# Second layer's weight sums carried over into its first half tile, next-y sums moved, products reordered

## The chip, the core and the metric

The kernel runs on one core of a Trainium2 chip. The metric is the device time of one execution in microseconds (us), lower is better. PE is the matmul engine (PEld its weight loads), DVE the vector engine, ACT the scalar engine, POOL the GpSimd engine, and SP issues most transfers; POOL issues the rest. Each engine works through its own queue in order, so an instruction that waits holds up everything behind it on that engine.

## The reference

```python
def _attn_ref(q, k, v, phi):
    a = softmax(phi over the sequence)                # 4 x 8 heads, 576 tokens, 32 memory slots
    k_m, v_m = a^T k, a^T v                           # 32 x 64 each
    attn = softmax(q k_m^T / sqrt(64))
    return attn v_m

x = attn_out as (2304 tokens, 512)
h = maximum(x @ w_in, 0);  x = (h * h) @ w_out        # 512 -> 2048 -> 512
h = x @ w_in2;  g = h * tanh(softplus(h))             # 512 -> 2048
out = g @ w_out2                                      # 2048 -> 512
```

All inputs and the output are float32. So is the arithmetic: a product is made of a high part and a low part (high by high, high by low, low by high), three matmuls each.

## The kernel before

**Layer one** (up to some 411 us) has four batches `b` of two halves with 288 tokens each; a *tile* is one (b, half) and runs over 16 chunks `fc` of the hidden width in `a_tile`, in parts for the first two batches. A *step* is one chunk: six matmuls into a bank `h`, `Relu` and `Square` on ACT, a high copy `g` and the subtraction that gives its low part on DVE (L594), and, three steps later, twelve matmuls `a` of an earlier chunk. Around them, the attention of coming batches is computed in small pieces.

**Weights of layer two.** They arrive as raw words of 64 bits, 32 units (`i2` 0 to 15, then `o2` 0 to 15). The class `Fold` turns a pair of units into seven *weight sums*, each split into high and low, staged in a tile `st` and written to memory as `wf_i2` or `wf_o2` by a transfer from POOL's queue (L301). Per unit: a load from SP (L251), a `Prelu` on ACT (L264) and two bit operations on DVE (L280, L282). Per pair: some sums on DVE, and seven times a cast on ACT (L299, `st`) with a subtraction on DVE (L300). `fold.tick` is called once per chunk; it starts a unit at every second call and does two pieces (`steps.pop`) per call. `EARLY` = 22 units are prepared before the pool `Y` is closed. The rest is done in the last two tiles, and whatever is left is drained in a loop before layer two's pools are opened. A `Prelu` is placed behind the last `Relu` of the program so far (`marks["step"]`); nothing else of `Fold` is tied. The framework's scheduler sets the order of all instructions on each engine.

**Layer two** takes three groups `i` of 768 tokens (two halves of 384). It multiplies by a scheme with seven products in place of eight. In a group's *first half* 56 steps (`h_step`, six matmuls of 384 columns into `hb`; line names `ht`, `hu`, `hs`, `a` on ACT and DVE) give the hidden values after `Mish`; in its *second half* 56 steps (`b_step`, nine matmuls of 256 columns) form the seven products `j` = 0 to 6 over eight pages `k`. `cast_step` makes high and low operands (`oph`, `opl`; L1008, L1009) three steps ahead; for `j` = 0 and 4 it also makes the operand of a later product on POOL at once (L1011, L1013). Each step reads one weight sum `u`, loaded by SP (L909) into 8 buffers (16 in the second halves), in the order in which `units` lists them. `y_work` prepares the next group's input: four loads `yr` (L858), four sums on POOL (L871, L876, L880, L885) and seven pairs of casts (L863, L864), two pieces per product of the second half in the program's text.

The *hinge* below is the passage from layer one's last matmul (411.37 us) into layer two's first half.

## Time and profile before

| | us |
|---|---|
| three runs | 788.3, 791.06 (median), 792.9 |
| profiled execution, first to last instruction | 788.8 |
| PE busy in it | 739.4 |
| mean granted clock of PE | 0.974 of full |

The profile names no time around the span; the span lies within the three runs, 2.3 us under their median. An engine's idle time is read from the timeline, where the number in brackets is the idle time before an instruction and the name behind it is what ended it.

### The profile page before, as it was taken

The numbers are of one execution on the slowest core, as the hardware profiler recorded it, in microseconds if no ns is written. First come the engines' busy times: TensorE is split into PE (matmuls) and PEld (weight loads), VectorE is DVE, ScalarE is ACT, GpSimd is POOL, SyncE is SP. The second block draws the span as 40 slices with busy tenths as digits, with TensorE's granted clock in tenths as the row PEclk, the third lists the DMA queues.
The fourth block names the chain that finished last, engine by engine and source line by source line (L and its number), as shares of the span: only waits on it lengthen the run. The fifth ranks groups of instructions, "written<-read, shape, count | busy, mean of one in ns | idle before, by whom it ended". The sixth has DMA issues, their size and how long they took to land.

```text
span 788.8 us, 16341 instructions
## 1 busy us (share of the span) xinstructions
PE 739.4 (94%) x5984; PEld 700.1 (89%) x5984; DVE 526.0 (67%) x1072; ACT 427.3 (54%) x960; POOL 136.3 (17%) x176
## 2 busy tenths in 40 slices
PE   5699999999899999989996799999999999999997
PEld 4488898998778888889995799899999999999997
DVE  3979846455757678768884559774558784556683
ACT  3577856565656677756654236452436552434552
POOL 0000000011111112232232414240112140111040
PEclk8699999999999999999998999999999999999999
DMA  9992535039888676786779978789788889788881
GB/s 333 406 406 72 187 100 195 28 124 299 279 294 297 214 246 220 258 341 208 290 254 343 295 247 292 240 268 301 240 262 251 247 265 303 244 258 251 247 265 62
DMA packets 89440, 195.85 MB, mean 248 GB/s; under 512 B 9872, under 2 KB 22672, under 8 KB 89360
## 3 DMA queue, kind: packets, MB, share of 16 engines
q1 hardware_dynamic: 80400, 165.45, 64.1%
q0 software_dynamic: 8960, 29.37, 9.6%
q8 instruction: 47, 0.77, 0.4%
q14 instruction: 33, 0.27, 0.1%
HBM read 151.78 MB, written 42.99 MB: 247 GB/s over the span
## 4 chain that ended last, share of the span: by engine, by line
PE 57%; issue 24%; POOL 7%; DMA 5%; DVE 3%; ACT 3%; SPq 1%; POOLq 0%; DVEq 0%; ACTq 0%
PE hb L964 7%; PE hb L965 7%; PE hb L966 7%; POOL wf_o L301 3%; POOL wf_i L301 3%; PE a L540 3%; PE a L541 3%; PE a L542 3%; DMA raw_i<-in_moe_w_in_dram 2%; PE h L578 1%; PE h L580 1%; PE h L579 1%; PE pw L478 1%; DMA wf_o<-st 1%; DMA u<-wf_i 1%
## 5 line engine op out<-in xcount | busy, mean ns | idle before, releaser
L540 PE MATMUL a<-g,o1h 128*128 128x288 f32 x512 | 150.5, 302 | 2.5 <-DVE ys L555 1.9
L541 PE MATMUL a<-g,o1l 128*128 128x288 f32 x512 | 149.0, 299 | 0.0
L542 PE MATMUL a<-g,o1h 128*128 128x288 f32 x512 | 132.5, 298 | 4.8 <-DVE g L594 4.8
L1009 DVE TENSOR_TENSOR opl<-a,oph 128x384 fp32r<-128x384 f32 x144 | 101.2, 723 | 50.8 <-ACT oph L1008 50.5
L964 PE MATMUL hb<-ych,u 128*128 128x384 f32 x336 | 114.8, 342 | 11.8 <-ACT ht L979 7.5
L965 PE MATMUL hb<-ycl,u 128*128 128x384 f32 x336 | 114.3, 340 | 0.0
L966 PE MATMUL hb<-ych,u 128*128 128x384 f32 x336 | 111.2, 340 | 0.0
L1008 ACT CAST oph<-a 128x384 fp32r<-128x384 f32 x144 | 73.5, 513 | 66.0 <-PE b20b L1030 5.9
L540 PEld LDWEIGHTS a<-g,o1h 128*128 128x128 f32 x512 | 97.2, 190 | 8.7 <-ACT s L586 2.9
L542 PEld LDWEIGHTS a<-g,o1h 128*128 128x128 f32 x512 | 90.3, 190 | 8.6 <-DVE g L594 6.3
L541 PEld LDWEIGHTS a<-g,o1l 128*128 128x128 f32 x512 | 97.5, 191 | 0.4 <-issue 0.4
L970 ACT ACTIVATE a<-hs 128x384 f32<-128x384 f32 x72 | 37.6, 525 | 92.2 <-DVE hs L974 92.2
L578 PE MATMUL h<-ah,wp 128*128 128x288 f32 x256 | 80.6, 316 | 5.8 <-ACT wp L484 2.8
L586 ACT ACTIVATE s<-h 128x288 f32<-128x288 f32 x128 | 52.2, 410 | 56.3 <-PE h L580 52.1
L301 POOL DMA_DIRECT2D wf_i<-st x56 | 30.3, 543 | 285.5 <-DVE st L300 278.6
L580 PE MATMUL h<-ah,wp 128*128 128x288 f32 x256 | 76.4, 299 | 0.7 <-DVE wp L485 0.7
L579 PE MATMUL h<-al,wp 128*128 128x288 f32 x256 | 76.7, 300 | 0.3 <-DVE al L468 0.3
L964 PEld LDWEIGHTS hb<-ych,u 128*128 128x128 f32 x336 | 64.3, 191 | 13.0 <-ACT ht L979 7.9
L594 DVE TENSOR_TENSOR g<-s,g 128x288 fp32r<-128x288 f32 x128 | 57.3, 450 | 26.4 <-ACT g L591 25.3
L974 DVE TENSOR_TENSOR hs<-hu,hb 128x384 f32<-128x384 f32 x72 | 39.5, 552 | 46.2 <-PE hb L966 45.8
L578 PEld LDWEIGHTS h<-ah,wp 128*128 128x128 f32 x256 | 48.7, 191 | 18.4 <-ACT s L586 5.3
L965 PEld LDWEIGHTS hb<-ycl,u 128*128 128x128 f32 x336 | 64.1, 191 | 0.0
(255 smaller groups left out, 1747.8 us busy)
## 6 DMA issues: line engine op xcount, KB each, us to landing
u<-wf_i SPq DMA_DIRECT2D x168, 256.0 KB, 3.7
u<-wf_o SPq DMA_DIRECT2D x168, 256.0 KB, 3.2
...
wf_i<-st POOLq DMA_DIRECT2D x56, 256.0 KB, 4.8
wf_o<-st POOLq DMA_DIRECT2D x56, 256.0 KB, 5.3
...
```

What stands on the lines that cost most here:

```text
L301: nc.gpsimd.dma_start(wf[key][k, :, j], st.bitcast(F32).rearrange("p s o -> p (s o)"))
L540: nc.tensor.matmul(o, wh[:, c, cs], sh, start=first, stop=False)
L541: nc.tensor.matmul(o, wl[:, c, cs], sh, start=False, stop=False)
L542: nc.tensor.matmul(o, wh[:, c, cs], sl, start=False, stop=last)
L578: nc.tensor.matmul(ph, w[:, 0, hg, fs], hi[:, hg], start=(hg == 0), stop=False)
L579: nc.tensor.matmul(ph, w[:, 0, hg, fs], lo[:, hg], start=False, stop=False)
L580: nc.tensor.matmul(ph, w[:, 1, hg, fs], hi[:, hg], start=False, stop=(hg == 1))
L964: nc.tensor.matmul(ps, wh, yh[:, d], start=(j < 4 and d == 0), stop=False, **kw)
L965: nc.tensor.matmul(ps, wh, yl[:, d], start=False, stop=False, **kw)
L966: nc.tensor.matmul(ps, wl, yh[:, d], start=False, stop=end, **kw)
L1008: nc.scalar.copy(hi, x)
L1009: sub(lo, x, hi.bitcast(F32))
```

## The change

1. `EARLY` goes from 22 to 18 units. `Fold.tick` counts time in steps (`now`) and starts a unit only if its load was recorded at least `AGE` = 4 steps ago. It does one piece per call in the first tiles, then one and two in turn, where it did two.
2. Every instruction of `tick` on every engine is placed behind the last `Relu` (or, in layer two, the last `Mish`) and the last subtraction that makes a low part (`marks["step"]`, `marks["lo"]`).
3. The staging tiles of the middle tiles come from three tags in place of two.
4. The loop that drained `Fold` before layer two is gone. The open units are ticked once per step of the first half of group 0 (0.43 steps of time each), with a small new pool `cs` for staging.
5. The `u` loads are placed behind each other in the order of `units`, with the `yr` loads between them. In group 0 the loads of the next y come after steps 8, 10, 12 and 14, three of its sums after steps 24, 29 and 34 of the first half, and its casts (with the fourth sum) at every fourth step of the second half, each tied behind that step's casts.
6. The products run in the order 0, 3, 1, 2, 4, 5, 6; the output of product 3 is added up at the end of product 2. The subtractions on POOL are put off by `k` steps. Big output tiles come from a new pool `bo`.

```diff
-EARLY = 22
+EARLY = 18
+AGE = 4.0
+PROD = [0, 3, 1, 2, 4, 5, 6]
...
+        def landed(self):
+            key, u = self.order[self.started]
+            return self.now - self.when[key, u] >= AGE
+
-        def tick(self, start=True):
+        def tick(self, start=True, pops=2, took=1.0):
+            self.now += took
+            with behind(marks, "step"), behind(marks, "lo"):
+                self.work(start, pops)
+
+        def work(self, start, pops):
             todo, self.bits = self.bits, []
-            if start and self.started < self.loaded and len(self.steps) < 5:
+            if start and self.started < self.loaded and len(self.steps) < 5 and self.landed():
...
-            for _ in range(2):
+            for _ in range(pops):
                 if self.steps:
                     self.steps.pop(0)()
...
-                nc.vector.tensor_sub(sl, s, sh.bitcast(F32))
+                marks["lo"] = nc.vector.tensor_sub(sl, s, sh.bitcast(F32))
...
-    def stage_y(n):
-        return Y.tile([P, 2, 256], F32R, tag=f"ys{2 + n // 2 % 2}", name=f"st{n}", bufs=2)
+    def stage_y(half):
+        def f(n):
+            pool, tag = ((Y, "ys2"), (Y, "ys3"), (X, f"ys{1 - half}"))[n // 2 % 3]
+            return pool.tile([P, 2, 256], F32R, tag=tag, name=f"st{n}", bufs=2)
+        return f
...
-                    fold.tick(start=fc % 2 == 0)
+                    fold.tick(pops=1)
...
-            fold.tick(start=fc % 2 == 0)
+            fold.tick(pops=1 + fc % 2)
...
+        if i:
+            sums = [s for s, _ in (sum1, sum2, sum3)]
+            last = [c for _, c in (sum1, sum2, sum3)]
+            return work, sums, last + [
+                lambda: cast(2, r[0, 1]), lambda: (cast(4, r[1, 0]), sum4()),
+                lambda: cast(6, r[1, 1]), lambda: cast(5, r[1, 0])]
...
-        units += [("o2", k, j) for j in range(7) for k in range(NPG)]
+        units += [("o2", k, j) for j in PROD for k in range(NPG)]
...
-            nc.sync.dma_start(t.bitcast(F32).rearrange("p s o -> p (s o)"), wf[key][k, :, j])
+            with behind(marks, "unit" if n else None):
+                marks["unit"] = nc.sync.dma_start(
+                    t.bitcast(F32).rearrange("p s o -> p (s o)"), wf[key][k, :, j])
...
-    while fold.busy():
-        fold.tick()
     flush()
     run_pend(0)
-    close(cm_cv)
...
+    cm_cs, CS = open_pool("cs", "right")
+    def stage_cs(n):
+        pool, tag, bufs = (CS, "stg2", 2) if n % 5 in (1, 3) else (CV, "stg", 3)
...
         if j == 0:
-            nc.gpsimd.tensor_sub(x, g[k, "x1"], x)
+            at(k, lambda: nc.gpsimd.tensor_sub(x, g[k, "x1"], x))
...
+            if j == 2:
+                tmp["u3"] = big("bu3")
+                each(add, tmp["u3"], tmp["u2"])
+                x, y = banks[3]
+                each(add, t, tmp["u3"])
...
+            if i == 0 and fold.busy():
+                assert step < 40
+                fold.tick(pops=1, took=0.43)
+            if step == 0 and more:
+                loads, sums, casts = y_work(i + 1, in_g("yr", 4), in_g("yt", 2))
+            if more and 8 <= step < 16 and step % 2 == 0:
+                loads.pop(0)()
+            if more and step in (24, 29, 34):
+                sums.pop(0)()
...
-            if one == two == 0 and (i + 1) * TT < NTOK:
-                work = y_work(i + 1, in_g("yr", 4), in_g("yt", 2))
-            if two % 3 == 2 and work:
-                work.pop(0)()
+            if more and 18 <= step < 46 and step % 4 == 2:
+                casts.pop(0)()
```

What it moves, at three places. **The hinge, ACT.** `ys312` is the last copy out of layer one's banks, `st` are casts of weight sums, `ht000` and `ht010` free layer two's first banks. Before:

```order
L557 COPY ys312_5551<-a3102_4940 128x288
L299 CAST st104_5227<-ct_o2_12_5057 128x256
L299 CAST st108_5373<-raw_o2_15_5060 128x256
L299 CAST st105_5331<-ct_o2_14_5262 128x256
L299 CAST st111_5461<-ct_o2_14_5262 128x256
L299 CAST st107_5368<-raw_o2_15_5060 128x256
L299 CAST st109_5424<-raw_o2_15_5060 128x256
L299 CAST st110_5428<-ct_o2_14_5262 128x256
L979 COPY ht000_5572<-hb000_5565 128x384
```

And with the change:

```order
L568 COPY ys312_5504<-a3102_4858 128x288
L1010 COPY ht000_5527<-hb000_5520 128x384
L310 CAST st103_5529<-ct_o2_12_5306 128x256
L1010 COPY ht010_5634<-hb010_5627 128x384
L1001 ACT_TABLE_LOAD
L1001 ACTIVATE a1100_5583<-hb000_5520 128x384
L1039 CAST oph53_6215<-a1100_5583 128x384
L1001 ACTIVATE a2200_5593<-hs003_5569 128x384
L1001 ACTIVATE a1101_5704<-hb010_5627 128x384
L1039 CAST oph54_6230<-a1101_5704 128x384
L310 CAST st105_5589<-ct_o2_14_5572 128x256
```

Seven casts stood between `ys312` and `ht000`; none does now, and the last pair's seven (105 to 111) follow spread over the steps up to about the 24th.

**The hinge, SP.** `u` with numbers under 56 are the weight sums of the running first half, those from 56 on belong to the second half, `yr` are loads of the next y. Before (`u57`, `u59`, `u61` and `u63` stand just ahead):

```order
L909 DMA u65_6241<-wf_o2_103 128x512
L909 DMA u67_6245<-wf_o2_103 128x512
L909 DMA u16_5665<-wf_i2_102 128x512
L909 DMA u69_6249<-wf_o2_103 128x512
L909 DMA u71_6253<-wf_o2_103 128x512
L858 DMA yr100_6300<-y1_104 128x2x384
L909 DMA u17_5679<-wf_i2_102 128x512
```

And with the change:

```order
L934 DMA u15_5643<-wf_i2_102 128x512
L875 DMA yr100_5659<-y1_104 128x2x384
L934 DMA u16_5661<-wf_i2_102 128x512
L934 DMA u17_5679<-wf_i2_102 128x512
L875 DMA yr101_5694<-y1_104 128x2x384
L934 DMA u18_5696<-wf_i2_102 128x512
L934 DMA u19_5708<-wf_i2_102 128x512
L875 DMA yr111_5718<-y1_104 128x2x384
```

The eight loads of the second half's weights are gone from here; they now stand behind `u55`.

**Layer one, DVE.** `ct_i2_6` and `ct_i2_4` are first bit operations on freshly loaded units, `g..` with `s..` makes a step's low part, `x20` belongs to the attention. Before, around chunk 15 of tile (1, 0):

```order
L447 STREAM_TRANSPOSE x20_2636<-psc20_2623 128x288 x2
L449 TENSOR_REDUCE smx20_2639<-x20_2636 128x18
L451 TENSOR_TENSOR x20_2636<-x20_2636,smx20_2639 128x576
L280 TENSOR_SCALAR ct_i2_6_3049<-raw_i2_6_2729 128x512
L594 TENSOR_TENSOR g10_15_2578<-s10_15_2577,g10_15_2578 128x288
L485 TENSOR_TENSOR wp20_2662<-pw200_2653,wp20_2662 128x512
```

And with the change, where the next pair begins, around chunk 13 of tile (1, 1):

```order
L605 TENSOR_TENSOR g11_12_2709<-s11_12_2708,g11_12_2709 128x288
L325 TENSOR_TENSOR ct_i2_2_2337<-raw_i2_3_2246,ct_i2_2_2337 128x256
L311 TENSOR_TENSOR st10_2807<-raw_i2_3_2246,st10_2807 128x256
L605 TENSOR_TENSOR g11_13_2763<-s11_13_2762,g11_13_2763 128x288
L469 TENSOR_TENSOR x20_2617<-x20_2617,ssm20_2712 128x576
L291 TENSOR_SCALAR ct_i2_4_2849<-raw_i2_4_2340 128x512
L332 TENSOR_TENSOR ct_i2_2_2337<-ct_i2_2_2337 128x256
L311 TENSOR_TENSOR st11_2855<-raw_i2_3_2246,st11_2855 128x256
```

Unit 6 was touched in chunk 15 of tile (1, 0), two units ahead of the one that was being finished; now unit 4 is touched four chunks later, behind the step's own subtraction.

**The second half of group 0, POOL.** `a110.` are the operands of product 1, `a120.` those of product 6, `yr`/`yt` with first figure 1 or 2 the sums of group 1's and group 2's y. Before:

```order
L1011 TENSOR_TENSOR a1104_5947<-x104_6008,a1104_5947 128x384
L885 TENSOR_TENSOR yr110_6482<-yr110_6482,yt12_6615 128x768
L871 TENSOR_TENSOR yt21_8159<-yr201_7948,yr200_7895 128x768
L1011 TENSOR_TENSOR a1105_6030<-x105_6091,a1105_6030 128x384
L1011 TENSOR_TENSOR a1106_6113<-x106_6174,a1106_6113 128x384
L876 TENSOR_TENSOR yt22_8210<-yr211_8030,yt21_8159 128x768
L880 TENSOR_TENSOR yr201_7948<-yr211_8030,yr201_7948 128x768
L1011 TENSOR_TENSOR a1107_6196<-x107_6302,a1107_6196 128x384
```

And with the change:

```order
L1044 TENSOR_TENSOR a1204_5986<-a1204_5986,a1104_5961 128x384
L899 TENSOR_TENSOR yr110_5743<-yr110_5743,yt12_5926 128x768
L1044 TENSOR_TENSOR a1205_6069<-a1205_6069,a1105_6045 128x384
L1044 TENSOR_TENSOR a1206_6152<-a1206_6152,a1106_6128 128x384
L1044 TENSOR_TENSOR a1207_6244<-a1207_6244,a1107_6211 128x384
L1042 TENSOR_TENSOR a1110_7233<-x110_7296,a1110_7233 128x384
L889 TENSOR_TENSOR yt21_7482<-yr201_7310,yr200_7283 128x768
L893 TENSOR_TENSOR yt22_7542<-yr211_7334,yt21_7482 128x768
```

All eight operands of product 1 are now made ahead of any y sum of the second half, and group 2's sums stand in group 1's first half.

## Rows read from the trace of the kernel before

**Rows 1.** The page, part 1: busy us of each engine, share, instructions.
```profile
PE 739.4 (94%) x5984; PEld 700.1 (89%) x5984; DVE 526.0 (67%) x1072; ACT 427.3 (54%) x960; POOL 136.3 (17%) x176
```

**Rows 2.** Windows: stretch, length, busy time by engine, granted clock, transfer share, GB/s.
```profile
200.00:360.00 160.00, 149.57 (x1342) 134.18 (x1341) 114.07 (x277) 102.88 (x263) 35.04 (x65) 0.98 0.76 264
...
560.00:580.00 20.00, 20.00 (x116) 20.00 (x115) 11.52 (x24) 7.06 (x14) 2.04 (x2) 1.00 0.79 244
```

**Rows 3.** PE's timeline at the hinge: start, length, instruction, idle before.
```profile
423.72 0.69 PE L964 MATMUL hb<-ych,u 128*128 128x384 f32 x1 [7.54 <-ACT ht L979]
...
436.22 0.41 PE L964 MATMUL hb<-ych,u 128*128 128x384 f32 x1 [2.10 <-DMA u<-wf_i]
...
440.39 0.41 PE L964 MATMUL hb<-ych,u 128*128 128x384 f32 x1 [1.84 <-DMA u<-wf_i]
```

**Rows 4.** ACT's timeline at the hinge.
```profile
422.88 0.40 ACT L299 CAST st<-ct_o 128x256 fp32r<-128x256 f32 x1 [2.00 <-DMA wf_o<-st]
423.19 0.86 ACT L979 COPY ht<-hb 128x384 f32<-128x384 f32 x2
```

**Rows 5.** SP's timeline at the hinge: issues in a row.
```profile
414.11 2.81 SPq L909 DMA_DIRECT2D u<-wf_i  x4
416.97 7.66 SPq L909 DMA_DIRECT2D u<-wf_o  x6
426.04 0.32 SPq L909 DMA_DIRECT2D u<-wf_i  x1
426.45 4.56 SPq L909 DMA_DIRECT2D u<-wf_o  x2
```

**Rows 6.** Windows of 4 us at the hinge, columns as in the windows above.
```profile
424.00:428.00 4.00, 4.00 (x14) 4.00 (x15) 2.67 (x6) 2.75 (x6) 0.54 (x1) 0.55 1.05 410
440.00:444.00 4.00, 3.61 (x14) 3.64 (x15) 3.08 (x3) 1.17 (x3) 4.00 (x3) 0.66 1.04 390
```

**Rows 7.** PE's timeline in layer one, with idle before.
```profile
209.11 1.30 PE L542 MATMUL a<-g,o1h 128*128 128x288 f32 x4 [1.88 <-DVE g L594]
229.36 0.40 PE L540 MATMUL a<-g,o1h 128*128 128x288 f32 x1 [1.50 <-DVE ys L555]
...
344.40 0.40 PE L542 MATMUL a<-g,o1h 128*128 128x288 f32 x1 [2.37 <-DVE g L594]
```

**Rows 8.** DVE's and ACT's timelines just ahead of those gaps.
```profile
208.26 0.43 DVE L280 TENSOR_SCALAR ct_i<-raw_i 128x512 int32<-128x512 int32 x1 [3.11 <-DMA raw_i<-in_moe_w_in_dram]
...
343.12 0.40 ACT L299 CAST st<-ct_o 128x256 fp32r<-128x256 f32 x1 [2.29 <-DMA wf_o<-st]
```

**Rows 9.** Windows: group 0's second half, then group 1's.
```profile
479.50:545.50 66.00, 63.10 (x517) 62.36 (x517) 50.13 (x71) 31.43 (x62) 21.98 (x15) 1.00 0.85 270
602.50:664.60 62.10, 62.10 (x517) 62.10 (x516) 44.67 (x71) 31.18 (x62) 17.80 (x12) 1.00 0.86 268
```

**Rows 10.** Timelines of DVE, POOL and PE in group 0's second half.
```profile
481.98 0.95 DVE L864 TENSOR_TENSOR ycl<-yr,ych 128x768 fp32r<-128x768 f32 x1
...
485.44 0.54 DVE L974 TENSOR_TENSOR hs<-hu,hb 128x384 f32<-128x384 f32 x1
485.91 2.15 DVE L864 TENSOR_TENSOR ycl<-yr,ych 128x768 fp32r<-128x768 f32 x1
...
485.27 1.97 POOL L871 TENSOR_TENSOR yt<-yr,yr 128x768 f32<-128x768 f32 x1 [0.17 <-DMA yr<-y]
...
492.03 0.39 PE L1031 MATMUL b01bg<-u,opl 128*128 128x256 f32 x1 [1.21 <-DVE opl L1009]
```

**Rows 11.** Groups by line, 300 to 412 us: name, count, busy us, mean ns.
```profile
L299 ACT CAST st<-raw_o 128x256 fp32r<-128x256 f32 x29 | 12.0, 424 | 7.8 <-DMA wf_o<-st 7.0 <-DVE raw_o L282 0.7
L300 DVE TENSOR_TENSOR st<-raw_o,st 128x256 fp32r<-128x256 f32 x27 | 11.0, 418 | 3.4 <-ACT st L299 3.4
```

**Rows 12.** The page, part 6: a load with KB each, us to landing.
```profile
u<-wf_i SPq DMA_DIRECT2D x168, 256.0 KB, 3.7
```

More of the change, by code (lines that the diff above doesn't have):

```diff
@@ L205, in fields @@
                 else:
-                    x[3] = X.tile([P, 512], F32, tag="ct", name=f"ct_{key}_{u}", bufs=2)
+                    x[3] = Y.tile([P, 512], F32, tag="ct", name=f"ct_{key}_{u}", bufs=2)
                 nc.vector.tensor_scalar(
@@ L240, in __init__ @@
             self.loaded = self.started = 0
-            self.raw, self.bits, self.odd, self.steps = {}, [], {}, []
-            self.pool, self.stage, self.n = None, None, 0
+            self.raw, self.bits, self.steps, self.when = {}, [], [], {}
+            self.pool, self.stage, self.n, self.now = None, None, 0, 0.0
         def load(self, n=1):
@@ L252, in load @@
                 self.raw[key, u] = t
+                self.when[key, u] = self.now
                 self.loaded += 1
@@ L275, in fields @@
             if u % 2 == 0:
-                t = X.tile([P, 512], F32, tag="ct", name=f"ct_{key}_{u}", bufs=2)
+                t = self.pool.tile([P, 512], F32, tag="ct", name=f"ct_{key}_{u}", bufs=2)
             else:
@@ L783, in body, with tick2, f @@
     drain(lanes)
-    def tick2(fc):
-        if fc == LAG + 1:
-            fold.stage = stage_y
-        fold.tick(start=fc % 2 == 0)
+    def tick2(half):
+        def f(fc):
+            if fc == LAG + 1:
+                fold.stage = stage_y(half)
+            fold.tick(pops=1 + fc % 2)
+        return f
     b, nb = 2, 3
@@ L845, in f @@
                 extra[0] = f"ys{1 - half}"
-            fold.tick(start=fc % 2 == 0)
+            fold.tick(pops=1 + fc % 2)
         return f
@@ L857, in load @@
             c0 = i * TT + n * HT
-            nc.sync.dma_start(r[k, n], y1[:, 2 * k:2 * k + 2, c0:c0 + HT])
+            with behind(marks, "unit" if i else None):
+                nc.sync.dma_start(r[k, n], y1[:, 2 * k:2 * k + 2, c0:c0 + HT])
         def cast(j, x):
@@ L862, in cast, with t1, t2, t3 @@
                 Y2.tile([P, 2, HT], F32R, tag=f"yc{part}{j}", name=f"yc{part}{i}{j}") for part in "hl")
-            nc.scalar.copy(hi, x)
-            nc.vector.tensor_sub(lo, x, hi.bitcast(F32))
+            with behind(marks, "hi" if i else None), behind(marks, "lo" if i else None):
+                nc.scalar.copy(hi, x)
+                nc.vector.tensor_sub(lo, x, hi.bitcast(F32))
         sub = nc.vector.tensor_sub if i == 0 else nc.gpsimd.tensor_sub
         work = [lambda k=k, n=n: load(k, n) for k, n in ((0, 0), (0, 1), (1, 1), (1, 0))]
-        def sum1():
+        def t1():
             r["t1"] = tmp(f"yt{i}1")
             sub(r["t1"], r[0, 1], r[0, 0])
-            cast(0, r[0, 0])
-        def sum2():
+        def t2():
             r["t2"] = tmp(f"yt{i}2")
             sub(r["t2"], r[1, 1], r["t1"])
-            cast(3, r["t1"])
-        def sum3():
+        def t3():
             sub(r[0, 1], r[1, 1], r[0, 1])
-            cast(1, r["t2"])
         def sum4():
-            cast(4, r[1, 0])
             sub(r[1, 0], r[1, 0], r["t2"])
-        return work + [
-            sum1, sum2, sum3, lambda: cast(2, r[0, 1]), sum4,
+        sum1 = t1, lambda: cast(0, r[0, 0])
+        sum2 = t2, lambda: cast(3, r["t1"])
+        sum3 = t3, lambda: cast(1, r["t2"])
+        if i:
[4 more added lines that the diff above has]
+                lambda: cast(6, r[1, 1]), lambda: cast(5, r[1, 0])]
+        both = [lambda s=s, c=c: (s(), c()) for s, c in (sum1, sum2, sum3)]
+        return work + both + [
+            lambda: cast(2, r[0, 1]), lambda: (cast(4, r[1, 0]), sum4()),
             lambda: cast(6, r[1, 1]), lambda: cast(5, r[1, 0])]
@@ L931, in body @@
     close(cm_wo)
+    cm_cs, CS = open_pool("cs", "right")
     cm_g, G = open_pool("g", "left")
+    def stage_cs(n):
+        pool, tag, bufs = (CS, "stg2", 2) if n % 5 in (1, 3) else (CV, "stg", 3)
+        return pool.tile([P, 2, 256], F32R, tag=tag, name=f"st{n}", bufs=bufs)
+    fold.stage = stage_cs
+    big_pool = [None]
     O, L = acc_tags, ["acc0", "acc1", "acc2", "acc3"]
@@ L969, in mish @@
             g[k, name] = half_tile(f"{name}_{k}", f"{name}{i}{k}", 1)
-            nc.scalar.activation(g[k, name], x, AF.Mish)
+            marks["step"] = nc.scalar.activation(g[k, name], x, AF.Mish)
         def total(name, a):
             t = half_tile("hs", f"hs{m}", 3)
-            add(t, a, ps)
+            marks["lo"] = add(t, a, ps)
             at(1, lambda: mish(name, t))
@@ L1039, in big @@
         def big(tag, bufs=1):
-            return G.tile([P, 3 * 256], F32, tag=tag, name=f"{tag}{m}", bufs=bufs)
+            return big_pool[0].tile([P, 3 * 256], F32, tag=tag, name=f"{tag}{m}", bufs=bufs)
         def store(t, a, b):
@@ L1067, in body @@
         plan += [("h", i, k, j) for k in range(NPG) for j in range(7)]
-        plan += [("b", i, j, k) for j in range(7) for k in range(NPG)]
+        plan += [("b", i, j, k) for j in PROD for k in range(NPG)]
     AHEAD = 3
     banks, tmp, g = {}, {}, {}
-    work = []
     def in_g(tag, bufs):
@@ L1077, in body @@
         feed(now + (8 if now < 56 else 16))
+        step = now % 56
+        more = (i + 1) * TT < NTOK
         if kind == "h":
             h_step(i, one, two, banks, tmp, g)
-        else:
+            if i == 0 and fold.busy():
[7 more added lines that the diff above has]
+                sums.pop(0)()
+        else:
+            if now == 56:
+                close(cm_cs)
+                close(cm_cv)
+                cm_bo, big_pool[0] = open_pool("bo", "right")
             b_step(i, one, two, banks, tmp)
-            if one == two == 0 and (i + 1) * TT < NTOK:
-                work = y_work(i + 1, in_g("yr", 4), in_g("yt", 2))
-            if two % 3 == 2 and work:
-                work.pop(0)()
+            if more and 18 <= step < 46 and step % 4 == 2:
+                casts.pop(0)()
         run_queue()
@@ L1090, in body @@
     close(cm_g)
+    close(cm_bo)
     close(cm_y2)
```

24 lines of the change are left out of this document (10 added, 14 removed).

## The prediction

> **What bounds the kernel now.** I read the page first: PE is busy 739.4 of 788.8 us [rows 1], so only idle PE time and time at a reduced clock can be won. Next comes a table of windows over the whole span, which tells where that time lies. Up to the first weight sums of layer two the order of instructions is the same on every engine, so the start stays as it is. From 200 to 360 us PE is busy 149.57 of 160 us at a mean granted clock of 0.98 [rows 2]. At the hinge it waits long and runs slow after it [rows 3, 6]. Group 0's second half takes 66.0 us, group 1's, with as many matmuls, 62.1 [rows 9]. In the steady part of layer two PE is busy all the time, 116 matmuls in 20 us, or 0.172 us each and 1.03 us per step of six [rows 2]; nothing is to be won there. The timeline of PE with idle time in brackets then names what ended each wait, and the timelines of ACT, DVE, POOL and SP say what that engine did ahead of it.
>
> **The hinge: what goes.** PE stands still 7.54 + 2.10 + 1.84 = 11.48 us [rows 3]. The first wait is for the copy `ht`, which starts at 423.19 because a cast `st` stood ahead of it on ACT until then, waiting 2.00 us for its staging buffer, that is for a transfer of an earlier sum [rows 4], and it was not the first cast that did. The two others are for loads `u<-wf_i`: from 416.97 to 431.0 SP issued eight loads of `wf_o`, which cannot start until their sums are written, and only one load that PE needed next [rows 5]. After these waits the granted clock was 0.55 in 424 to 428 and 0.66 in 440 to 444, with PE busy 4.00 and 3.61 us [rows 6]: 4.00 x 0.45 + 3.61 x 0.34 = 3.0 us more. **Loss 14.5 us.** The change takes both causes away: no cast stands between the last copy and `ht000`, and the eight loads stand behind `u55`.
>
> **The hinge: what comes.** The last pair's work now runs beside the first 24 steps, some 25 us. On ACT these are 7 casts at 0.42, 2.9 us; on DVE 7 subtractions at 0.42 and four bit operations and four sums on as many or twice as many numbers, so at most 0.84 each, 9.7 us at most [rows 11]; on POOL seven issues, none waited for, since `wf_o` is read only from step 56 on. DVE is busy 11.52 and ACT 7.06 in 20 us of the steady first half [rows 2]: over 25 us DVE comes to 14.4 + 9.7 = 24.1, ACT to 8.8 + 2.9 = 11.7. Both fit, DVE barely. For transfers: by step 25 the loads `u11` to `u25` (15 x 0.262 MB), some ten staged sums (2.6), two stores of y1 (0.6) and four loads of y (1.6) must be through, 8.7 MB in 25.8 us, or 337 GB/s, where 390 and 410 were moved over 4 us [rows 6]. They fit as well, without room. So the cover is thin in one place: `u11` is issued only behind the stores of y1, which is where the group at 414.11 stood, 2.7 us after layer one's last matmul [rows 5]. It is wanted six steps after that matmul, at about 6 to 7 us; landing takes 3.7 us at the median [rows 12], more in a crowd. I charge 0.5 us for the copies out of layer one's banks, 1.5 for `u11` and its followers, 1 for DVE: 3.0 us. Below it lies 0.5; above, 8.8, which is the 264 GB/s of 200 to 360 us [rows 2] in place of 337: 8.7 MB then take 33 us, 7 late, and 1.8 of clock. I take the small value, since the crowd at the hinge itself reached 390. **Gain 11.5.**
>
> **Layer one.** Idle time from 200 to 360 us is 160 - 149.57 = 10.4, and the clock costs 149.57 x 0.02 = 3.0 [rows 2]. Three gaps make 5.75 of it [rows 7]. At 209.11 and 229.36 DVE stood in a first bit operation on a unit whose load had not landed (3.11 us at 208.26), with the step's own subtraction queued behind it; at 344.40 ACT stood in a cast whose staging buffer was not free, 2.29 us at 343.12 [rows 8]. The change starts a unit four steps after its load, some 9.3 us (18 matmuls of 288 columns each, at 288/384 of 0.172 us), and places its work behind the step's; the staging ring grows from four to six tiles in the middle tiles, and in the tile of the third gap the casts leave free the four chunks into which the eight loads of `u` fall. So 1.88 + 2.37 go, and with them the clock's 3.0, which in finer windows lies right behind these two: 7.25. The gap of 1.50 I leave in place: it lies at the start of tile (2, 0), whose attention now ends a step later, with its low part right ahead of the copies out of the banks; it may vanish or grow by 1.3. Of the other 4.7 us, much belongs to the attention's chains, which stay; I take 1.75. For waits that appear elsewhere, as every piece now has a fixed place in a queue, I charge 1.0. **Gain 8.0**, between 0 (every wait returns at another step) and 11.
>
> **Group 0's second half.** 66.0 - 62.1 = 3.9 us [rows 9]. POOL's sum of group 2's y (1.97 us at 485.27) and the next two stood ahead of operands of product 1, which PE waited for three times, 1.21 us the longest [rows 10], 2.90 together. While that sum ran, DVE's `ycl` with two inputs from on-chip memory took 2.15 us against 0.95 alone, but `hs`, which reads a bank, still 0.54 [rows 10]. The order now gives product 1's operands ahead of all these sums, and product 3 fills eight steps in between. **Gain 2.9**, bounds 1.5 and 3.9.
>
> The Trainium skill (SBUF — State Buffer, section "SBUF: two separate sides") says that GpSimd and VectorE share a pair of ports as an exclusive lock, held for a whole instruction, against VectorE operations with two SBUF inputs. The trace agrees, by `ycl` and `hs` above, and the rule speaks against point 5: three sums in a first half cost DVE up to 3 x (2.15 - 0.95) = 3.6 us there. In group 1's first half DVE has room for that (11.52 of 20 us). In group 0's the same three sums ran before, but without the last pair's work beside them; now DVE would come to 24.1 + 3.6 = 27.7 us in 25, which is a way into the second rival.
>
> **What costs nothing.** The order of products moves no matmul; the two additions of product 3 move to the end of product 2, eight steps before a bank of theirs is written again. Zero, 1 us either way. The casts of y (0.95 on DVE) move from the end of the first half into the products, where DVE is busy 44.67 of 62.1 us [rows 9]. Putting off POOL's subtractions costs nothing while they end two products ahead of use. The end, after the last matmul, is the same.
>
> **The sum.** 11.5 + 8.0 + 2.9 = 22.4 us, from 788.8 to 766.4 for an execution like the profiled one. That one lies 2.3 us under the median of the three runs, 791.06; from the median the sum gives 768.7, which is my forecast: **768.7**.
>
> **The rivals.**
> 1. *The forecast*: 763 to 774. For it: each cause removed has its wait in brackets, and the order shows it gone. Chance 0.62.
> 2. *Layer two's start is bound by DVE or by transfers.* Loads or `hs` come late in the first 25 steps. For it: 337 GB/s wanted, DVE at 24.1 of 25 us. Against it: 390 to 410 was moved, and two banks' worth of steps, seven, lie between a bank's end and its reuse. The hinge then keeps about 8.8 us in place of 3.0: 768.7 + 5.8 = 774.5. Chance 0.15.
> 3. *Layer one's waits return.* Casts wait for buffers or units at other steps; that term is 0: 776.7. With the second rival, 782.5. For it: one wait of about 2 us brings the slow clock with it, as at the hinge [rows 3, 6]. Chance 0.11.
> 4. *Slower.* Units' loads land later than four steps, in the tiles in which now up to 1.5 pieces a step sit in DVE's queue; each late load costs what the one at 208.26 did, 1.88 and 1.5 of clock, 3.4 us. The gain of 22.4 is gone from seven late loads on; at ten of the 32 the time is 768.7 + 34 = 802.7. Against it: even without regard to landing, two late loads stopped PE for 1.5 us and more [rows 7, 8]. Chance 0.04.
> 5. *It does not do what it says.* The scheduler might put the work back into the same places: 791. The order of the built program speaks against it at each of the three places. Chance 0.05, with all that comes out near no change.
> 6. *All goes*, and the hinge keeps 0.5: 14.5 - 0.5 + 11 + 3.9 = 28.9, 762.2. Chance 0.03.
>
> **How the numbers follow.** 768.7 is the likeliest case's. The range 760 to 780 takes in the cases 1, 2, 3 (each alone) and 6, 0.62 + 0.15 + 0.09 + 0.03 = 0.89 on paper, of which I believe 8 in 10, since the unknown costs are many. Half a per cent, about what a measurement of this kernel tells from no change, is 4 us: faster than 787 are cases 1, 2, 3 and 6, 0.91; the same 0.05; slower 0.04.
>
> **What would show it.** In the profile after: no idle PE time over 2 us between 395 and 440, and a granted clock of 1.00 there; ACT's `ht` copies right behind the last `ys`; SP without `wf_o` loads before the first half's end; no window of 200 to 360 with a clock under 1.00; group 0's second half at about 62.5 us. Wrong would be: gaps of 2 us before `u<-wf_i` or behind DVE at the hinge (rival 2), casts on ACT that wait for transfers of earlier sums ahead of a `Relu` (rival 3), first bit operations that wait for loads (rival 4).

## The result, and the profile after

The changed kernel takes **769.88 us** (median of four runs, 768.32 to 771.89), the kernel before 791.98 us (four runs, 788.30 to 793.17): ratio 0.971, 95 % interval 0.967 to 0.975. The forecast was 768.7 us, range 760 to 780. The profiled execution spans 767.9 us, before 788.8. The total was right; one of its three terms was not.

A table made from the two traces shows where the time went. A stage ends with its last matmul; "products" is a group's second half, from its first product matmul to its last; 516 matmuls start in it each time, 504 of them its own and twelve left over from the first half. The change places the loads, sums and casts of the next y in group 1 as it does in group 0.

| stage, us | before | after | gain | predicted |
|---|---|---|---|---|
| start, to three eighths of the `a` matmuls (three of eight tiles) | 174.47 | 174.22 | 0.25 | 0 |
| rest of layer one | 236.91 | 225.96 | 10.95 | 8.0 |
| hinge, to the first product matmul | 68.12 | 56.90 | 11.22 | 11.5 |
| products, group 0 | 66.23 | 65.25 | 0.98 | 2.9 |
| first half, group 1 | 56.70 | 56.70 | 0 | 0 |
| products, group 1 | 62.37 | 65.23 | -2.86 | 0 |
| group 2 | 119.09 | 119.08 | 0 | 0 |
| after the last matmul | 4.91 | 4.60 | 0.3 | 0 |
| sum | 788.8 | 767.9 | 20.85 | 22.4 |

The page of after, part 1, and windows with busy time of PE, PEld, DVE, ACT and POOL, granted clock, share of transfers and GB/s; they answer to [rows 1, 2, 6, 9]:

```profile
PE 735.2 (96%) x5984; PEld 697.3 (91%) x5984; DVE 530.3 (69%) x1072; ACT 424.1 (55%) x960; POOL 132.1 (17%) x176
...
200.00:360.00 160.00, 155.53 (x1414) 141.53 (x1415) 127.69 (x313) 111.57 (x291) 41.83 (x77) 1.00 0.81 285
...
416.00:420.00 4.00, 1.75 (x11) 1.44 (x10) 4.00 (x6) 1.43 (x3) 3.91 (x5) 1.00 1.06 394
420.00:424.00 4.00, 4.00 (x16) 4.00 (x15) 3.97 (x4) 1.72 (x4) 3.82 (x4) 0.57 1.02 381
...
457.07:522.32 65.25, 63.46 (x518) 62.63 (x518) 47.21 (x72) 33.76 (x66) 15.00 (x12) 1.00 0.88 284
579.02:644.25 65.23, 63.45 (x518) 62.65 (x518) 47.16 (x72) 33.77 (x66) 14.99 (x12) 1.00 0.83 258
700.94:763.33 62.39, 62.39 (x517) 62.19 (x516) 39.28 (x65) 29.32 (x59) 12.81 (x11) 1.00 0.68 212
```

Layer one's stretch is busy 155.53 of 160 us at full clock, where it was 149.57 at 0.98. Groups 0 and 1 both have 1.8 us of idle PE in their products, and PE's records there are 1.1 us longer; group 2, which prepares no next y, has no idle time.

The timelines at the hinge, PE, ACT and SP in turn, and the loads of `u<-wf_i` issued there (the last line is their time to landing):

```profile
418.97 0.44 PE L995 MATMUL hb<-ych,u 128*128 128x384 f32 x1 [2.25 <-DMA u<-wf_i]
...
399.54 0.70 ACT L568 COPY ys<-a 128x288 f32<-128x288 f32 x2 [0.68 <-PE a L553]
400.13 0.50 ACT L1010 COPY ht<-hb 128x384 f32<-128x384 f32 x1
...
401.22 4.16 SPq L934 DMA_DIRECT2D u<-wf_i  x5
405.43 0.43 SPq L875 DMA_DIRECT2D yr<-y  x1
...
L934 SPq DMA_DIRECT2D u<-wf_i x18: 319/320/627, 391.9 to 417.7; - x18
...
DMA to landing us min/median/max: 3.1/6.3/8.0
```

The three waits of [rows 3], 11.48 us, have become one of 2.25 us. `ht` stands right behind the last `ys`; no `wf_o` load stands among SP's before 452.06. The wait that is left ends with a load in a crowd: at the median such a load took 6.3 us here, 3.7 over the page [rows 12].

The groups of waits from 200 us to layer one's end (engine, waiting line, what ended it: us in all, times, longest). Before, 200 to 411:

```profile
DVE ct_i L280 <- DMA raw_i<-in_moe_w_in_dram: 11.9, 5, 3.1
ACT st L299 <- DMA wf_o<-st: 11.2, 9, 2.6
ACT raw_o L264 <- DMA raw_o<-in_moe_w_out_dram: 10.4, 5, 4.1
...
ACT st L299 <- DMA wf_i<-st: 6.3, 4, 3.3
```

After, 200 to 400, and then the two gaps on PE that are left, with the cast on ACT behind the first:

```profile
ACT st L310 <- DMA wf_o<-st: 6.9, 7, 1.7
...
ACT st L310 <- DMA wf_i<-st: 4.2, 2, 3.2
...
ACT raw_o L275 <- DMA raw_o<-in_moe_w_out_dram: 1.7, 1, 1.7
...
231.32 0.40 PE L551 MATMUL a<-g,o1h 128*128 128x288 f32 x1 [1.51 <-ACT g L602]
...
235.52 0.40 PE L551 MATMUL a<-g,o1h 128*128 128x288 f32 x1 [0.99 <-ACT g L602]
...
230.04 0.42 ACT L310 CAST st<-raw_i 128x256 fp32r<-128x256 f32 x1 [3.25 <-DMA wf_i<-st]
```

No wait of DVE for a raw unit is left in this list, and casts wait 11.1 us for staging where they waited 17.5. Only the first of the two gaps has such a cast behind it; ahead of the second, ACT stood 1.68 us in an operation of the attention that waited for DVE (at 234.46).

Last, group 1's product 4 on DVE, POOL and PE:

```profile
620.70 5.23 DVE L1040 TENSOR_TENSOR opl<-a,oph 128x384 fp32r<-128x384 f32 x4
...
620.86 2.09 POOL L899 TENSOR_TENSOR yr<-yr,yt 128x768 f32<-128x768 f32 x1 [0.90 <-DVE ycl L882]
622.90 3.89 POOL L1044 TENSOR_TENSOR a<-a,a 128x384 f32<-128x384 f32 x3
...
623.41 0.39 PE L1062 MATMUL b10mm<-u,opl 128*128 128x256 f32 x1 [0.79 <-DVE opl L1040]
...
628.13 0.39 PE L1062 MATMUL b12acc<-u,opl 128*128 128x256 f32 x1 [0.82 <-DVE opl L1040]
```

This is the new wait. POOL's fourth sum of y holds back three subtractions of product 4, and the four run in a row. Meanwhile DVE needs 5.23 us for four `opl`, 1.31 each, where a step is 1.07 us (nine matmuls at 58.79 / 495 us, from the windows of e9 below); elsewhere one takes 0.56.

### The profile page after: what moved, and what is told of

The parts are those of the page before. It is cut to its first block, busy times and chain, and to the rows that moved or that the text cites. A ratio compares the mean times of both kernels' runs of the same rounds, so it can differ in the third digit from the quotient of the medians.

```text
span 767.9 us, 16335 instructions
## 1 busy us (share of the span) xinstructions
PE 735.2 (96%) x5984; PEld 697.3 (91%) x5984; DVE 530.3 (69%) x1072; ACT 424.1 (55%) x960; POOL 132.1 (17%) x176
## 4 chain that ended last, share of the span: by engine, by line
PE 71%; issue 8%; DVE 7%; DMA 7%; ACT 4%; POOL 2%; SPq 0%; DVEq 0%; POOLq 0%; ACTq 0%
PE hb L995 7%; PE hb L996 7%; PE hb L997 7%; PE a L551 6%; PE a L553 5%; PE a L552 5%; PE h L589 3%; PE h L590 2%; PE h L591 2%; DMA raw_i<-in_moe_w_in_dram 2%; POOL wf_o L312 2%; PE pw L489 1%; DVE opl L1040 1%; DMA u<-wf_i 1%; DMA wf_i<-st 1%
## 5 line engine op out<-in xcount | busy, mean ns | idle before, releaser
L1040 DVE TENSOR_TENSOR opl<-a,oph 128x384 fp32r<-128x384 f32 x144 | 97.1, 690 | 47.4 <-ACT oph L1039 47.2
L995 PE MATMUL hb<-ych,u 128*128 128x384 f32 x336 | 113.8, 339 | 2.2 <-DMA u<-wf_i 2.2
L589 PE MATMUL h<-ah,wp 128*128 128x288 f32 x256 | 79.1, 310 | 5.1 <-ACT wp L495 3.1
L591 PE MATMUL h<-ah,wp 128*128 128x288 f32 x256 | 76.0, 297 | 0.7 <-DVE wp L496 0.7
L995 PEld LDWEIGHTS hb<-ych,u 128*128 128x128 f32 x336 | 63.5, 189 | 2.9 <-DMA u<-wf_i 2.6
L997 PEld LDWEIGHTS hb<-ych,u 128*128 128x128 f32 x336 | 63.4, 189 | 0.0
```

The lines of the kernel that those rows point to most:

```text
L589: nc.tensor.matmul(ph, w[:, 0, hg, fs], hi[:, hg], start=(hg == 0), stop=False)
L591: nc.tensor.matmul(ph, w[:, 1, hg, fs], hi[:, hg], start=False, stop=(hg == 1))
L995: nc.tensor.matmul(ps, wh, yh[:, d], start=(j < 4 and d == 0), stop=False, **kw)
L997: nc.tensor.matmul(ps, wl, yh[:, d], start=False, stop=end, **kw)
L1040: marks["lo"] = sub(lo, x, hi.bitcast(F32))
```

## The experiments

Ten kernels were run. Their times come from three sittings, in which the kernel before had medians of 791.9 (e1 to e4), 794.9 (e5 to e8) and 793.3 us (e9, e10), so small differences are read from the stages of the traces:

| kernel | median us | ratio to before, interval | rest of layer one | hinge | products 0 | products 1 |
|---|---|---|---|---|---|---|
| after | 769.88 | 0.971, 0.967-0.975 | 225.96 | 56.90 | 65.25 | 65.23 |
| e1 | 774.70 | 0.978, 0.972-0.983 | 227.77 | 60.41 | 65.03 | 65.24 |
| e2 | 773.63 | 0.978, 0.973-0.982 | 224.75 | 60.12 | 66.78 | 65.29 |
| e3 | 786.54 | 0.994, 0.991-0.996 | 235.69 | 62.54 | 65.26 | 65.24 |
| e4 | 768.88 | 0.971, 0.966-0.975 | 225.94 | 56.71 | 64.98 | 64.95 |
| e5 | 764.55 | 0.964, 0.960-0.968 | 226.14 | 56.86 | 63.63 | 63.38 |
| e6 | 766.66 | 0.967, 0.963-0.971 | 225.80 | 54.50 | 65.20 | 65.01 |
| e7 | 763.26 | 0.962, 0.957-0.966 | 225.80 | 54.08 | 63.61 | 63.64 |
| e8 | 758.60 | 0.956, 0.953-0.960 | 222.34 | 53.77 | 63.61 | 63.64 |
| e9 | 756.87 | 0.954, 0.951-0.958 | 222.37 | 54.68 | 62.37 | 62.39 |
| e10 | 766.12 | 0.966, 0.963-0.969 | 225.00 | 53.94 | 65.16 | 65.21 |

**e3, layer one as before.**

```diff
-EARLY = 18
+EARLY = 22
...
-            with behind(marks, "step"), behind(marks, "lo"):
-                self.work(start, pops)
+            if self.tied:
+                with behind(marks, "step"), behind(marks, "lo"):
+                    self.work(start, pops)
+            else:
+                self.work(start, pops)
...
-            fold.tick(pops=1 + fc % 2)
+            fold.tick(start=fc % 2 == 0)
```

(`tied` is set only ahead of layer two; where it isn't, a unit starts without regard to its load, and the middle tiles stage in two tags.)

> The changed kernel with layer one's weight sums as before: 22 early units, no four steps between load and start, two pieces a step, no ties, four staging tiles; as the work is done earlier, the last pair is finished ahead of layer two, as before. Loads of u stay in order. Theory: layer one ends some 11 us later (last matmul at 411 instead of 400.2 us), with casts waiting for staging and first bit operations waiting for raw loads, and the wait for the copy ht is back, the waits for u are not: 769.9 + 11.2 + 5.2 = 786 us (783 to 789). Rival, by the sizes of the prediction (layer one 8.0): 783 us. Rival, layer one's gain came from elsewhere: its last matmul stays near 400 us and the time under 777 us.

786.54 us, as the theory said. Layer one takes 235.69 us, so the number of early units, the four steps, the pieces per call, the ties and the staging are together worth 9.7 of its 10.95 us; they were not taken apart, and the other 1.2 were not located. Its first large gap is the one of [rows 7] again (1.81 us, ended by DVE's `g`, at 210.0). With the pair finished ahead of layer two, the wait for `ht` is back; ACT, PE and a window of e3:

```profile
421.99 0.40 ACT L315 CAST st<-ct_o 128x256 fp32r<-128x256 f32 x1 [1.90 <-DMA wf_o<-st]
422.30 0.86 ACT L1015 COPY ht<-hb 128x384 f32<-128x384 f32 x2
...
422.82 0.69 PE L1000 MATMUL hb<-ych,u 128*128 128x384 f32 x1 [6.90 <-ACT ht L1015]
...
424.00:428.00 4.00, 4.00 (x14) 4.00 (x13) 1.78 (x4) 2.66 (x6) 0.00 (x0) 0.50 0.75 268
```

No wait of over 0.5 us for a `u` follows it. So the hinge had two causes: with the casts back and the loads in order it takes 62.54 us, before, with the loads out of order as well, 68.12, and with neither 56.90: some 5.6 us each. The casts' share is net of the wait at 416.73, which goes when they come back. The loads' share is a difference between kernels that differ elsewhere in layer two as well, and e10 below shows that one of those edits changes the hinge by 3.0 us; so it is not shown by itself.

**e1, the last pair finished first.**

```diff
+    while fold.busy():
+        fold.tick()
     flush()
     run_pend(0)
```

> The changed kernel (769.9 us) with one thing undone: the loop that finishes the last pair's weight sums before layer two stands there again; the loads of u stay in order. Theory, two causes at the hinge: the casts ahead of the copy ht are one, so a wait of 5 to 8 us before the first ht copies comes back, with some 1.7 us at the lower clock behind it, while the present wait of 2.25 us for a load and the 1.7 us of clock behind that go: 769.9 + 7.5 + 1.7 - 4.0 = 775 us (773 to 778). Rival, the order of the loads was the whole cause and the casts would have been hidden: 766 to 770.5 us.

774.7 us, the number of the theory, by other shares. PE's waits and windows:

```profile
408.75 0.69 PE L997 MATMUL hb<-ych,u 128*128 128x384 f32 x1 [2.80 <-ACT ht L1012]
...
414.06 0.66 PE L997 MATMUL hb<-ych,u 128*128 128x384 f32 x1 [1.11 <-DMA u<-wf_i]
...
408.00:412.00 4.00, 3.25 (x10) 3.25 (x11) 2.79 (x6) 3.29 (x7) 0.54 (x1) 0.50 1.05 401
412.00:416.00 4.00, 2.89 (x9) 2.42 (x9) 1.12 (x2) 1.38 (x3) 0.00 (x0) 0.50 1.02 379
```

The wait for `ht` is 2.80 us, not 5 to 8, since the tied casts come in a shorter row; but the clock stays at half through both windows, (3.25 + 2.89) x 0.5 = 3.1 us, and a load is still late. Layer one itself is 1.8 us longer.

**e2, loads untied.**

```diff
-            with behind(marks, "unit" if n else None):
+            with behind(marks, None):
                 marks["unit"] = nc.sync.dma_start(
```

(And the same for `yr`.)

> The changed kernel with one thing undone: loads of u and of the next y are tied to nothing, so eight loads of the second half's weights stand between those that the first half needs. Theory: they cannot start before their sums are written, and these are now written during the first half's first steps, so PE waits for u again, as before at 436.22 and 440.39 (1.84 to 2.10 us each, two or more of them) with clock behind it: 774 to 782 us. Rival, the ties are worth nothing once no drain stands ahead: 768 to 771 us, and the next y's loads, which come earlier, make no wait of their own.

773.63 us: the hinge grows by 3.2 us, the lower end of the theory, but not by its mechanism. The wait for a load is 0.95 us. The long one is for DVE; PE, then POOL and DVE ahead of it:

```profile
419.02 0.69 PE L995 MATMUL hb<-ych,u 128*128 128x384 f32 x1 [2.61 <-DVE hu L1016]
...
410.75 1.84 POOL L893 TENSOR_TENSOR yt<-yr,yt 128x768 f32<-128x768 f32 x1 [0.49 <-PE hb L997]
412.54 2.01 POOL L896 TENSOR_TENSOR yr<-yr,yr 128x768 f32<-128x768 f32 x1
...
410.81 2.06 DVE L320 TENSOR_TENSOR raw_o<-raw_o,ct_o 128x256 f32<-128x256 f32 x1
412.79 2.37 DVE L311 TENSOR_TENSOR st<-raw_o,st 128x256 fp32r<-128x256 f32 x2
```

The untied loads of y land earlier, POOL's sums start at 408.4 in place of 414.7 (10.1 us after layer one's last matmul in place of 14.6), and operations of 0.42 us on DVE take up to 2.06 beside them. Group 0's products lose another 1.5 us: the loads of group 2's y come earlier too, and POOL's first sum of it now stands between the subtractions of product 4, where PE waits 1.40 and 0.77 us for `opl`: ```profile
498.25 1.85 POOL L889 TENSOR_TENSOR yt<-yr,yr 128x768 f32<-128x768 f32 x1 [0.48 <-DVE opl L1040]
```

What the order of the loads brings in the changed kernel is thus as much the late start of POOL's sums as the loads' own places.

**e4, products in the order 0 to 6.**

```diff
-PROD = [0, 3, 1, 2, 4, 5, 6]
+PROD = list(range(7))
```

(With the output of product 3 added up at its end.)

> The changed kernel with the products in the order 0 to 6, and the output of product 3 added up at its own end, as before. Theory: the order is worth nothing (the prediction's zero), and what group 1's second half lost against before (59.1 to 61.6 us from the last first-half matmul on) comes from POOL's fourth sum of y and the operands beside it in product 4: both stay, 769.9 us within 1.5. Rival, the order itself brings that loss, in groups 0 and 1: 764 us. Rival, product 3 in second place gives product 1's operands the time that group 0 lacked before: 772 to 773 us.

768.88 us, all stages within 0.3 us of after: the order of the products is worth nothing here, and with the sums in the first half product 1's operands come in time without it.

**e5, the fourth sum early.**

```diff
-            return work, sums, last + [
-                lambda: cast(2, r[0, 1]), lambda: (cast(4, r[1, 0]), sum4()),
+            return work, sums, [lambda: (cast(4, r[1, 0]), sum4())] + last + [
+                lambda: cast(2, r[0, 1]),
```

> The changed kernel with one thing moved: the cast of operand 4 of the next y and POOL's fourth sum behind it come first among the casts (step 18 of the second half) in place of fifth (step 34). Theory: in groups 0 and 1 that sum (2.09 us) holds up POOL's last three subtractions of product 4, and all four run in a row, for 6 us in which DVE's opl takes 1.31 us in place of 0.56, more than the 1.07 us of a step; PE waits for it (0.79, 0.17 and 0.82 us). Moved, both groups' second halves fall from 61.65 us (last first-half matmul to last product matmul) to near group 2's 58.8, which has no such sum: 769.9 - 5.7 = 764.2 us (763 to 766). Rival, the seven casts of y on DVE and ACT, tied behind the steps' own, are the cause, and the sum only stands beside them: 769 to 770.5 us. Rival, the sum does the same in product 1: the waits move there, 768 to 770 us.

764.55 us, the theory's number, but in part by luck: the products fall by 1.6 and 1.9 us, 3.5 of the expected 5.7, more than half of the 2.86 of each group. The profiled executions differ by 4.2 us, 0.9 of it at the start, where the kernels are alike. One wait of 0.72 to 0.82 us for `opl` is left in each group.

**e6, the next y later.**

```diff
-            if more and 8 <= step < 16 and step % 2 == 0:
+            if more and 22 <= step < 30 and step % 2 == 0:
-            if more and step in (24, 29, 34):
+            if more and step in (36, 40, 44):
```

> The changed kernel with the four loads of the next y after steps 22, 24, 26 and 28 (in place of 8, 10, 12, 14) and its three sums after steps 36, 40, 44 (in place of 24, 29, 34). Theory: the wait of 2.25 us at 416.73 and the 3.4 us at half clock behind it come from a crowd of transfers (share 1.04 to 1.06 of 16 engines in 412 to 420, a load of u landing 7.55 us after its issue at 411.38), in which the four loads of y have 1.6 MB; without them both go: 769.9 - 4.0 = 766 us (765 to 767.5). Rival, weight sums and loads of u fill the transfers by themselves: a wait of 1 to 2 us stays and the time is 768.5 to 770.5 us. Rival, the sums now run beside the products' first operands on DVE: 771 to 773 us.

766.66 us. The hinge falls by 2.4 us, and the windows answer to those of after above:

```profile
416.00:420.00 4.00, 4.00 (x25) 4.00 (x24) 4.00 (x12) 1.73 (x4) 2.63 (x5) 1.00 1.03 357
420.00:424.00 4.00, 3.62 (x21) 3.33 (x21) 2.94 (x8) 1.62 (x4) 1.99 (x3) 1.00 1.02 374
```

PE no longer waits in the first, and the clock is whole. The edit moves loads and sums at once. But the wait was for a load of `u`, and the loads of `u` that SP issues from layer one's end on land sooner; after (11 loads, issued in 401.2 to 411.4), then e6 (12, 403.9 to 415.0):

```profile
DMA to landing us min/median/max: 3.6/5.5/8.0
...
DMA to landing us min/median/max: 3.3/3.8/4.6
```

The share of transfers alone does not make the difference, since it is 0.93 to 1.03 in e6 too, from 404 to 420: the late landings go with the loads of y among those of `u`. What POOL's sums add was not told apart.

**e7, both edits.**

> The two edits together, the fourth sum early and the next y's loads and sums later. Theory: the two gains lie in different stages and add up: 769.9 - 5.7 - 4.0 = 760.2 us (758.5 to 763). Rival, the sums that were moved later and the fourth sum that was moved earlier meet on POOL in the first products: 764 to 767 us.

763.26 us, where 760.2 was expected and 764 the rival's. The stages say that the gains do add (hinge 54.08, products 63.6 each), but the expectation added the theories' 5.7 and 4.0 where the stages of e5 and e6 had shown 3.5 and 2.4: 769.9 - 5.9 = 764.0. In e7's stages the gains are 2.8 and 3.2, 6.0 us. So the sizes were wrong, and the rival's number is met without its mechanism. The profiled execution also lost some 2.4 us at 88 us against after, in code that is the same in all these kernels; up to three eighths of the `a` matmuls 1.0 us of it is left:

```profile
88.00:92.00 4.00, 2.30 (x13) 2.07 (x12) 2.98 (x8) 2.98 (x9) 0.00 (x0) 0.82 0.94 311
92.00:96.00 4.00, 4.00 (x36) 3.09 (x35) 2.17 (x5) 2.57 (x7) 0.00 (x0) 0.75 0.43 143
```

A raw unit landed later there than in after (ACT waited 1.47 us for it in place of 0.40); e3 and e6 waited 1.72 and 1.64 us there, with a low clock behind it too. Whether e7's other executions lost the same is not known, since only one is profiled.

**e8, e7 with a slower start of tile (2, 0).**

```diff
-            fold.tick(pops=1 + fc % 2)
+            fold.tick(pops=1 + (fc % 2 if half or fc > LAG + 1 else 0))
```

> The two edits, and in the first five chunks of tile (2, 0) one piece of a weight sum per chunk in place of one and two in turn. Theory: the two largest waits left in layer one (1.51 us at 229.81 and 0.99 us at 234.53) come from a cast on ACT that waits 3.25 us for a staging tile whose transfer takes 6.26 us; with fewer pieces there the ring of four tiles does not fill: the time of the run with both edits less 1.5 to 2.5 us, some 758 us. Rival, the transfers are late whatever the pieces: no difference.

758.60 us. Layer one falls by 3.5 us against e7, more than expected: the waits at 229.81 and 234.53 and a third of 0.7 at 280 are gone. In e8:

```profile
230.95 0.43 ACT L310 CAST st<-raw_i 128x256 fp32r<-128x256 f32 x1 [1.09 <-DMA wf_i<-st]
...
222.00:278.00 56.00, 55.80 (x544) 48.69 (x545) 44.28 (x104) 40.30 (x105) 13.60 (x25) 1.00 0.82 291
```

The cast still waits for its staging tile, 1.09 us in place of 3.25, but it comes one step later, behind the `g` (227.03) that it held up before, and PE does not notice.

**e9, e8 with all casts early** (and the fourth sum third among them).

```diff
-            if more and 18 <= step < 46 and step % 4 == 2:
+            if more and 10 <= step < 31 and step % 3 == 1:
```

> The kernel of the last run (next y later, fourth sum early, slow start of tile (2, 0); 758.6 us) with the seven casts of y, the fourth sum third among them, at steps 10, 13, ... 28 of the second half in place of 18, 22, ... 42, so that none lies beside product 4's subtractions on POOL. Theory: what is left over group 2's second half (60.04 against 58.79 us, with one wait of 0.82 us for opl in each of groups 0 and 1) comes from casts on DVE that read two on-chip inputs beside those subtractions (1.77 us in place of 0.94); it goes: 758.6 - 2.5 = 756.1 us (755 to 757). Rival, seven casts cost DVE this much wherever they lie, and the waits move to product 1 or 2: 758 to 760 us.

756.87 us, ratio 0.954: the best kernel here. From the last first-half matmul to the last product matmul, groups 0, 1 and 2 of e9:

```profile
455.40:514.19 58.79, 58.79 (x495) 58.79 (x494) 45.01 (x69) 32.16 (x63) 14.09 (x11) 1.00 0.90 298
574.48:633.28 58.80, 58.80 (x495) 58.80 (x494) 45.03 (x69) 32.13 (x63) 14.08 (x11) 1.00 0.85 266
693.57:752.36 58.79, 58.79 (x493) 58.59 (x492) 38.00 (x62) 27.71 (x56) 11.78 (x10) 1.00 0.66 207
```

All three are equal, PE busy throughout, with the same seven casts on DVE, each now 0.95 to 0.96 us long. The casts are free ahead of POOL's subtractions of product 4, and cost 1.25 us a group beside them; the fourth sum moved as well, but only from step 18 to step 16.

**e10, the next y's loads and sums in the second half again.**

```diff
-            if more and 8 <= step < 16 and step % 2 == 0:
-                loads.pop(0)()
-            if more and step in (24, 29, 34):
-                sums.pop(0)()
         else:
...
+            if more and 0 <= step < 8 and step % 2 == 0:
+                loads.pop(0)()
+            if more and step in (16, 20, 24):
+                sums.pop(0)()
             if more and 18 <= step < 46 and step % 4 == 2:
```

> The changed kernel with one thing undone: the next y's loads stand after steps 0 to 6 and its first three sums after steps 16, 20, 24 of the second half, ahead of its casts, as before the change; the order of the products and the subtractions that are put off stay. Theory: product 1's operands are ready on POOL ahead of the sums by the put-off order alone, so the three waits of group 0 before (2.90 us) do not return; the wait for a load at the hinge goes with the loads of y (2.4 us); the three sums beside casts on DVE cost 0 to 2 us per group: 767.5 to 771.5 us. Rival, by the prediction's step the sums' place is what brought the 2.9 us: both groups' second halves grow by 2.9, 769.9 - 2.4 + 5.8 = 773 us.

766.12 us, under the theory's 767.5: the products stay at 65.2 us, and the hinge falls by 3.0. POOL in e10's group 0, its last operand of product 1 and its first sum of y:

```profile
459.73 1.26 POOL L1042 TENSOR_TENSOR a<-x,a 128x384 f32<-128x384 f32 x1 [0.50 <-DVE opl L1040]
466.61 1.84 POOL L889 TENSOR_TENSOR yt<-yr,yr 128x768 f32<-128x768 f32 x1 [5.62 <-DMA u<-wf_o]
```

So against this place, the sums in the first halves, part 5 of the change, gained nothing in the products and cost 3.0 us at the hinge. "As before" holds for the program's text alone: in the trace of before, the scheduler had moved group 1's sums up into group 0's first half and group 2's into group 0's second half, which tied loads do not allow.

## Why the prediction was right, and where it was not

**The hinge: right in cause, place and size.** Both causes were named, and by e3 each is worth some 5.6 us of the 11.2; the casts are shown by e1 and e3, the loads by the waits of [rows 3], which e3 no longer has, while untying them alone (e2) brought other waits. The 3.0 us charged for what comes is what is left over: e8 and e10 reach 53.8 to 53.9 against 56.90. Its kind was misjudged. The 1.5 us for `u11` behind the stores of y1 did not come, since it was issued 1.05 us after layer one's last matmul and landed at 404.87; the wait is at 416.73, for a load issued at 411.38, with transfers at a share of 1.06 and DVE full beside POOL's sums. That is the second rival's mechanism, at a fraction of its price: 2.25 us idle and 4.00 x 0.43 = 1.7 of clock.

**Layer one: right in mechanism, too small.** The three gaps of [rows 7] and the clock of 0.98 are gone, 5.75 + 3.0 us. The prediction left the gap of 1.50 in place; one of 1.51 us does stand at the start of tile (2, 0), but it is another: the wait for DVE's copies went, and a cast's wait for staging came. For new waits it charged 1.0, and 1.51 + 0.99 came. What it under-rated is the term "1.75 of other 4.7": idle time besides these gaps fell from 4.7 us to 4.47 - 2.50 = 2.0, and 1.5 us were gained ahead of 200 us, outside the stretch that it added up. The third rival's mechanism, waits that return at other steps, is those 2.5 us, 1.51 of them behind a cast, which e8 removes. Its premise, that one wait of about 2 us brings the slow clock with it, did not hold for them (1.00 in 200 to 360).

**Products: the step that failed is "what costs nothing".** The waits for product 1's operands went, as said; but neither the order of the products (e4) nor the place of the sums in the first half (e10) is needed for it. In e10 the sums start 5.6 us after the last of these operands. That loads are tied, so that group 2's sums stay out of group 0's second half, fits e10 and e2; which edit did it is not shown, since no run undid the put-off subtractions, or two of these at once. And two things taken at zero cost 2.86 us in each of groups 0 and 1, which is why group 0 gained 1.0 and group 1 lost 2.86. The prediction hid the casts of y under "DVE is busy 44.67 of 62.1 us" [rows 9] and POOL's put-off subtractions under "two products ahead of use". Both covers are true as averages and false for the 6 us in which POOL's fourth sum and the subtractions run in a row. [rows 10] had the price, `ycl` 2.15 us in place of 0.95, and the prediction used it for the first half alone; `opl` reads on-chip memory twice as well. e5 and e9 put a number on each: 1.6 to 1.9 us for the sum, 1.25 for the casts.

**The total** came out 1.6 us off in the span by luck, because layer one's 3.0 too little and the products' 4.8 too much nearly cancel. It would be wrong to read the hit as proof of each term.

**The signs.** Held: `ht` behind `ys`, full clock in 200 to 360, no first bit operation that waits for a load there. Held in substance: the `wf_o` loads stand behind `u55`, but start at 452.06, 5.0 us ahead of the first product matmul. Not held: one idle time of over 2 us in 395 to 440 (2.25) with a clock of 0.57 behind it, and group 0's second half at 65.25 in place of 62.5. The signs of rivals 2 and 3 thus each showed once, the gap before `u<-wf_i` and the cast at 230.04, at a fraction of their price.

## What to carry to other kernels

Work that is moved under an engine that is "busy 70 % of the stage" must be placed against the few microseconds in which it lands, with the slower rate of operations beside another engine's. A piece that may wait for a buffer goes behind the work that the matmuls need, and starts only when its transfer can have ended. When a prediction hits its total, its stages still have to be compared one by one: here they showed 13 us more to win (e9).

## What the runs showed of the hardware

**DVE beside POOL.** While POOL computes, DVE's operations with two inputs from on-chip memory take 1.31 us for 0.56 (`opl`), 2.06 for 0.42 (a sum beside a POOL operation of 1.84 to 2.01); `hs`, which reads a bank, keeps 0.54 [rows 10]. POOL's own subtraction goes from 1.02 alone to 3.89 / 3 = 1.30. The Trainium skill (SBUF — State Buffer, section "SBUF: two separate sides") calls the shared port pair an exclusive lock for a whole instruction. These sizes agree with it in that DVE's operation grows by up to the length of one of POOL's (0.75 and 1.64 us), not by a fixed factor. They do not agree with two operations that never overlap: the four `opl`, the sum and the three subtractions shown above come to 4 x 0.56 + 2.04 + 3 x 1.02 = 7.3 us one by one (2.04 is the sum in e8), and ran in 6.1 us, from 620.70 to 626.79.

**The clock after a wait.** The 2.25 us before 418.97 were followed by 0.57 in 420 to 424; in e4 waits of 1.83 and 0.94 us at the same place were followed by none, and e1's 2.80 and 1.11 by half clock through both windows shown there. PE and clock of e4:

```profile
419.13 0.44 PE L995 MATMUL hb<-ych,u 128*128 128x384 f32 x1 [1.83 <-DMA u<-wf_i]
...
420.00:424.00 4.00, 3.06 (x18) 2.75 (x17) 4.00 (x3) 1.02 (x3) 3.98 (x5) 1.00 1.04 395
```

The length of the wait alone does not decide: PE's 1.70 us before 90.37 in e7 went with the 0.82 and 0.75 shown there, a shorter wait than e4's 1.83. What sets the one apart from the other was not tried; at the hinge the difference is worth the 1.7 us.
